# First weights in two halves on SyncE's queue, x tiles 3-4 behind them, and ScalarE's load of tiles 5-6 behind its dummy activation

## The chip, the cores and the metric

The kernel runs on one core of one Trainium2 chip. The metric is the device time of one execution in microseconds. Before the change it is 232.5 us, the median of three runs (232.27, 232.5 and 233.13).

## What is computed

```python
wg = w.reshape(G, M, D)                    # M = 4 weights of a group, along the rows of w
mag = jnp.abs(wg)
order = jnp.argsort(mag, 1)
thr = jnp.take_along_axis(mag, order[:, M - N:M - N + 1, :], 1)   # N = 2: the second largest
mask = (mag >= thr).astype(w.dtype)
wp = (wg * mask).reshape(D, D)
return jnp.einsum("bsd,df->bsf", x, wp) + b
```

x is 16 x 512 x 1024, w is 1024 x 1024, b has 1024 elements, all bf16. In each group of four weights the two of largest magnitude are kept, and x is multiplied by the weights that are left.

## The kernel before, in words

The 8192 rows of x are 64 tiles of 128 rows; w is two row groups g of 512 rows, each laid out as 128 partitions x 4 weights of a group x 1024 columns. Once the weights are pruned and spread into `wp_nat`, the rest of the kernel is plain: x arrives transposed by DMA (`load_nat`, L408), eight matmuls of 128x512 make half a tile of output, VectorE adds the bias and ScalarE's queue stores it.

The start is what the change touches. While the weights are still coming in, tiles 0 to 6 are worked on with the half of x that meets row group 0 (`load_x`, L103): their rows are loaded as they lie, TensorE transposes them four blocks to a tile (`transpose`, L188; the 28 matmuls of L193), ScalarE copies the result to SBUF (`copy_xt`, L196, line L198), and TensorE multiplies by the pruned pieces as they become ready (`mm_piece`, L213, line L229). VectorE prunes a piece in steps (`Piece.do`, L164, lines L169 and L159): the magnitudes (abs), the larger and smaller of each pair (hi, lo), two combinations (t1, t2), the threshold (thr), the mask, and the product (mult). For the first piece, 256 columns of row group 0, some steps stand in parts: abs0a and abs0b are its first and its last two weights of a group, hi0a and hi0b the same, p and q its column halves, y the last two weights, u and v the first and second.

The order on each engine is written out by hand: the lists `order` (L266) hold each engine's steps as tokens, `run` (L391) emits them, and `seq` (L67) chains each engine's instructions in program order. The TensorE list begins T3a T4a T5a T6a T2a, so the transposes of tiles 3, 4, 5, 6 and 2, eight of them for tiles 3-4, eight for 5-6 and four for 2; then come products of tiles 3 and 4 with the first piece, and tiles 0 and 1 are transposed later.

Ahead of the lists stand the loads (L118 to L129). A load is issued from SyncE ("SPq" in the profile, queue q1) or from ScalarE ("ACTq", queue q10). SyncE issues the first two weights of each group of the first piece, then x tiles 3-4, tile 2, the second piece, tiles 0-1 and further weights, and then a transposing DMA (`xlead`). ScalarE issues the last two weights of the first piece and x tiles 5-6. Behind these ScalarE runs a dummy activation into `spark` (L121), in front of which the compiler puts the load of the activation table. Every x or w load above has a semaphore; TensorE's first weight load of tiles 3-4 waits for that of tiles 3-4, and VectorE's two abs steps wait for one half of the first piece each.

TensorE runs fillers before T3a: `filler(6, 4)` makes six matmuls of 512 columns on constants, `filler(14)` fourteen of 128 columns (L404, L405; line L138 in the profile). Their result is not used.

Of the kernel before, what the change touches and what calls it, by code (L numbers as in the profile page):

```python
# [11 lines left out]
def kernel(  # L12
# [7 lines left out]
    nc = tc.nc  # L20
    P = 128
    bf16 = mybir.dt.bfloat16
# [3 lines left out]
    Act = mybir.ActivationFunctionType  # L26
# [28 lines left out]
    const = ctx.enter_context(tc.tile_pool(name="const", bufs=1))  # L55
# [11 lines left out]
    def seq(eng, inst):  # L67
        if eng in tails:
            tc.add_manual_dep(inst.ins, tails[eng].ins.name, NOSYNC, reason="program order")
        tails[eng] = inst  # L70
        return inst

    def pe(i):
        return seq("pe", i)
# [4 lines left out]
    def act(i):  # L79
        return seq("act", i)  # L80
# [4 lines left out]
    def pool(i):  # L85
        return seq("pool", i)

    spark = const.tile([P, 1], bf16)

    w_sb = const.tile([P, G, 4, Dout], bf16)  # L90
    wv = w.rearrange("(g q m) f -> q g m f", g=G, m=4)
    x_sb = {}
# [3 lines left out]
    def issue(eng, out_, in_):  # L96
        q = nc.sync if eng == "sp" else nc.scalar
        return seq(eng, q.dma_start(out_, in_))

    def load_w(g, c0, c1, ma=0, mb=4, eng="sp"):  # L100
        issue(eng, w_sb[:, g, ma:mb, c0:c1], wv[:, g, ma:mb, c0:c1])

    def load_x(ta, tb, eng="sp"):  # L103
        xs = const.tile([P, tb - ta, HK], bf16, name=f"x_{ta}")
        issue(eng, xs[:], xf[ta * P:tb * P, :HK].rearrange("(t p) k -> p t k", p=P))
        for t in range(ta, tb):
            x_sb[t] = xs[:, t - ta, :]
# [8 lines left out]
    xnat, held = {}, {}  # L116

    load_w(0, 0, 256, 0, 2)  # L118
    load_w(0, 0, 256, 2, 4, "act")
    load_x(5, 7, "act")  # L120
    act(nc.scalar.activation(spark[:], nc.const_aps.tensor(1.0, [P, 1], bf16), Act.Abs))  # L121
    load_x(3, 5)
    load_x(2, 3)
    load_w(0, 256, 512)
    load_x(0, 2)
# [10 lines left out]
    def filler(n, rep=1):  # L136
        for _ in range(n):
            pe(nc.tensor.matmul(warm_ps[:, :rep * P], lhsT=nc.const_aps.tensor(1.0, [P, P], bf16),  # L138
                                rhs=nc.const_aps.tensor(1.0, [P, rep * P], bf16), start=True, stop=True))
# [119 lines left out]
    def stage(key):  # L259
        solo = key[1] == "h"  # L260
        q, h, at = (pair_of[key[0]], key[2], int(key[0] != SOLO)) if solo else (key[0], key[1] // 2, key[1] % 2)
        if (q, h) not in staged:
# [12 lines left out]
        ),  # L275
        "dve": (
# [4 lines left out]
        ),  # L281
        "act": (
            "C3a C4a C5a C6a C2a S0b0 C0a C1a abs2 S3b0 S2b0 abs3 S0b1 U6h0 S3b1 S2b1 S0b2 S3b2 S2b2 S0b3 U6h1 S3b3 "
# [107 lines left out]
    def run(queues):  # L391
        while any(queues.values()):
            moved = False
            for eng, toks in queues.items():
                while toks and all(n in written for n in needs(eng, toks[0])):
                    emit(eng, toks[0])
                    tok = toks.pop(0)
                    written.add(tok)
                    if tok[0] == "M" or tok[0].islower():
                        written.update(atoms(tok))  # L400
                    moved = True
            assert moved, queues

    filler(6, 4)  # L404
    filler(14)  # L405
    run({eng: order[eng].split() for eng in order})

    def load_nat(ta, tb):  # L408
# [117 lines left out]
```

## Time and profile before

| | before |
|---|---|
| runs | 232.27, 232.5, 233.13 us |
| profiled execution | 232.89 us |
| its span, first to last instruction | 231.1 us |
| granted TensorE clock, mean | 1.000 |
| TensorE matmuls busy | 226.6 us |
| VectorE busy | 107.9 us |
| ScalarE busy | 14.0 us |
| DMA, mean | 165 GB/s |

All durations in what follows are of the profiled execution, and times are counted from its first instruction. A row of the timeline or of the chain gives start, length, engine, line, operation, output and input, and the number of merged instructions; a trailing bracket gives the idle time before and what ended it. A row of the DMA issues gives the count, the size, and the time from issue to landing. A row of a DMA queue gives packets, MB and the share of 16 engines' time. A row of the stretches gives the stretch, its length, then busy time and number of instructions of TensorE's matmuls, its weight loads, VectorE, ScalarE and GpSimd, then the granted clock, the share of the DMA engines and GB/s. Matmuls are pipelined: each shown length holds the pipeline's depth, so the pace is read from start to start.

### The profile page before, as it was taken

The numbers are of one execution on the slowest core, as the hardware profiler recorded it, in microseconds if no ns is written. First come the engines' busy times: TensorE is split into PE (matmuls) and PEld (weight loads), VectorE is DVE, ScalarE is ACT, GpSimd is POOL, SyncE is SP. The second block draws the span as 40 slices with busy tenths as digits, with TensorE's granted clock in tenths as the row PEclk, the third lists the DMA queues.
The fourth block names the chain that finished last, engine by engine and source line by source line (L and its number), as shares of the span: only waits on it lengthen the run. The fifth ranks groups of instructions, "written<-read, shape, count | busy, mean of one in ns | idle before, by whom it ended". The sixth has DMA issues, their size and how long they took to land.

```text
span 231.1 us, 2851 instructions
## 1 busy us (share of the span) xinstructions
PE 226.6 (98%) x1142; PEld 110.9 (48%) x1162; DVE 107.9 (47%) x200; ACT 14.0 (6%) x27; POOL 17.6 (8%) x15
## 2 busy tenths in 40 slices
PE   8999999999999999999999999999999999999995
PEld 5986444444444444444444444444444444444443
DVE  3999877844424424424424424423423423433434
ACT  2874100000000000000000000000000000000000
POOL 1000199700000000000000000000000000000000
PEclk9999999999999999999999999999999999999999
DMA  6999999997399422991259821693128932122122
GB/s 203 276 197 280 164 217 223 297 320 252 124 206 232 155 91 72 237 281 64 75 116 252 222 94 71 162 298 134 65 91 198 273 122 83 54 91 91 53 86 91
DMA packets 79308, 38.19 MB, mean 165 GB/s; under 512 B 64192, under 2 KB 71744, under 8 KB 79296
## 3 DMA queue, kind: packets, MB, share of 16 engines
q1 hardware_dynamic: 68384, 20.75, 43.6%
q10 hardware_dynamic: 10912, 17.27, 20.9%
q8 instruction: 9, 0.15, 0.3%
q14 instruction: 3, 0.02, 0.0%
HBM read 3.28 MB, written 16.78 MB: 87 GB/s over the span
## 4 chain that ended last, share of the span: by engine, by line
PE 98%; issue 0%; DVE 0%
PE ps L242 88%; PE ps L229 5%; PE tp L242 2%; PE ps L138 2%; PE tp L193 1%; PE ps L193 0%; DVE o L437 0%
## 5 line engine op out<-in xcount | busy, mean ns | idle before, releaser
L242 PE MATMUL ps<-wp_nat,xb 128*128 128x512 bf16 (+1 forms) x831 | 178.9, 375 | 0.9
L242 PEld LDWEIGHTS <-xb 128*128 128x128 bf16 x848 | 82.2, 98 | 97.7
L437 DVE TENSOR_TENSOR o<-ps,bias_sb 128x512 bf16<-128x512 f32 (+1 forms) x112 | 71.6, 677 | 113.7 <-PE ps L242 111.4
L433 POOL TENSOR_TENSOR st<-st,bias_sb 128x1024 f32<-128x1024 f32 x8 | 16.7, 2142 | 0.0
L242 PE MATMUL ps<-wp_nat,xlead 128*128 128x512 bf16 x63 | 14.7, 379 | 0.1
L242 PEld LDWEIGHTS <-xlead 128*128 128x128 bf16 x88 | 8.6, 98 | 10.2
L229 PE MATMUL ps<-wp,xt 128*128 128x256 bf16 (+1 forms) x130 | 12.8, 258 | 0.0
L439 DVE TENSOR_TENSOR o<-ps,st 128x512 bf16<-128x512 f32 x16 | 11.1, 691 | 2.8 <-PE ps L242 2.2
L229 PEld LDWEIGHTS <-xt 128*128 128x128 bf16 x130 | 10.9, 98 | 1.1
L242 PE MATMUL ps<-wp_nat,xlow 128*128 128x512 bf16 x47 | 10.6, 379 | 0.1
L264 ACT COPY st<-ps 128x512 f32<-128x512 f32 x14 | 7.4, 600 | 3.2 <-PE ps L229 3.1
L242 PEld LDWEIGHTS <-xlow 128*128 128x128 bf16 x48 | 4.7, 98 | 5.7
L159 DVE TENSOR_TENSOR mag<-mag,hi 128x256 bf16<-128x256 bf16 (+2 forms) x15 | 6.1, 435 | 0.1
L159 DVE TENSOR_TENSOR wp<-w_sb,mag 128x256 bf16<-128x256 bf16 (+2 forms) x15 | 6.1, 435 | 0.1
L242 PE MATMUL tp<-wp_nat,xlead 128*128 128x512 bf16 x23 | 5.8, 380 | 0.0
L138 PE MATMUL ps<-const-bfloat16-1.0 128*128 128x128 bf16 (+1 forms) x20 | 4.2, 408 | 0.8 <-PEq L510 0.8
L169 DVE TENSOR_SCALAR mag<-w_sb 128x512 uint16<-128x512 uint16 (+2 forms) x5 | 2.3, 473 | 3.5 <-DMA w_sb<-in_w_dram 3.5
L138 PEld LDWEIGHTS <-const-bfloat16-1.0 128*128 128x128 bf16 x20 | 2.3, 146 | 2.4 <-issue 2.4
L159 DVE TENSOR_TENSOR hi<-mag 128x512 bf16<-128x512 bf16 (+2 forms) x7 | 3.2, 458 | 0.1
L159 DVE TENSOR_TENSOR lo<-mag 128x512 bf16<-128x512 bf16 (+1 forms) x6 | 3.1, 509 | 0.0
L193 PEld LDWEIGHTS <-x 128*128 128x128 bf16 x28 | 2.3, 124 | 0.3 <-DMA x<-in_x_dram 0.2
L422 POOL COPY pruned<-wp 128x1 bf16<-128x1 bf16 x1 | 0.2, 187 | 26.7 <-DVE wp L159 26.7
(18 smaller groups left out, 18.8 us busy)
## 6 DMA issues: line engine op xcount, KB each, us to landing
out_dram<-o ACTq DMA_DIRECT2D x58, 256.0 KB, 2.4
wp_nat<-wp SPq DMA_DIRECT2D x14, 128.0 KB, 3.2
out_dram<-o ACTq DMA_DIRECT2D x10, 128.0 KB, 1.7
w_sb<-in_w_dram SPq DMA_DIRECT2D x2, 512.0 KB, 5.5
w_sb<-in_w_dram SPq DMA_DIRECT2D x3, 256.0 KB, 5.1
x<-in_x_dram SPq DMA_DIRECT2D x2, 256.0 KB, 4.3
x<-in_x_dram ACTq DMA_DIRECT2D x1, 256.0 KB, 4.0
bias_sb<-in_b_dram SPq DMA_DIRECT2D x1, 256.0 KB, 4.7
```

Of the source, the lines that this page charges most:

```text
L138: pe(nc.tensor.matmul(warm_ps[:, :rep * P], lhsT=nc.const_aps.tensor(1.0, [P, P], bf16), rhs=nc.const_aps.tensor(1.0, [P, rep * P], bf16), ...
L159: dve(nc.vector.tensor_tensor(out, a, b_, op=op))
L169: dve(nc.vector.tensor_single_scalar(mag.bitcast(u16), w_.bitcast(u16), 0x7FFF, op=Alu.bitwise_and))
L193: pe(nc.tensor.transpose(tp[:, m, :], xg[:, m, :], ident[:]))
L229: pe(nc.tensor.matmul(ps[:, c0 + d:c1 + d], lhsT=xpk[t][:, m, :], rhs=wp[:, g, m, c0:c1], start=(new and m == ms.start), stop=(left[key] = ...
L242: pe(nc.tensor.matmul(ps, lhsT=xt[:, kt - koff, :], rhs=wp_nat[:, kt, c0:c1], start=(kt == first), stop=(kt == last)))
L264: act(nc.scalar.copy(staged[(q, h)][:, at, :, :].rearrange("p t c -> p (t c)"), ps_open.pop(key)[:]))
L422: pool(nc.gpsimd.tensor_copy(out=pruned[:], in_=wp[:, 1, 3, Dout - 1:]))
L433: pool(nc.gpsimd.tensor_tensor(st[:], st[:], bias.to_broadcast([P, 2, 2, CW]), op=Alu.add))
L437: dve(nc.vector.tensor_tensor(o[:, c0:c1], ps, bias_sb[:, c0:c1], op=Alu.add))
L439: dve(nc.vector.tensor_tensor(o[:, c0:c1].rearrange("p (n c) -> p n c", n=2), ps.rearrange("p (n c) -> p n c", n=2), add, op=Alu.add))
```

## The change

The second half of the first piece's weights moves from ScalarE's queue to SyncE's, right behind the first half. Tiles 3-4 follow it on SyncE. ScalarE's first instruction becomes the dummy activation, which now writes one column of the tile that the load of tiles 5-6 fills; so that load waits for it. Three of the 14 short fillers go. VectorE works through abs, hi and lo of the first half before it waits for the second half, and its one lo step of 512 columns becomes two of 256.

```diff
-    spark = const.tile([P, 1], bf16)
...
     def load_x(ta, tb, eng="sp"):
         xs = const.tile([P, tb - ta, HK], bf16, name=f"x_{ta}")
+        if eng == "act":
+            act(nc.scalar.activation(xs[:, 0, :1], nc.const_aps.tensor(1.0, [P, 1], bf16), Act.Abs))
         issue(eng, xs[:], xf[ta * P:tb * P, :HK].rearrange("(t p) k -> p t k", p=P))
...
     load_w(0, 0, 256, 0, 2)
-    load_w(0, 0, 256, 2, 4, "act")
+    load_w(0, 0, 256, 2, 4)
+    load_x(3, 5)
     load_x(5, 7, "act")
-    act(nc.scalar.activation(spark[:], nc.const_aps.tensor(1.0, [P, 1], bf16), Act.Abs))
-    load_x(3, 5)
     load_x(2, 3)
...
         "dve": (
-            "abs0a abs0b hi0a lo0 hi0b t20 t10p t10q thr0p thr0q mask0yp ...
+            "abs0a hi0a lo0a abs0b hi0b lo0b t20 t10p t10q thr0p thr0q mask0yp ...
...
     filler(6, 4)
-    filler(14)
+    filler(11)
```

The rest of VectorE's list, and the lists of the other engines, stay as they are. The load of tiles 5-6 is the only one from ScalarE that `load_x` makes.

8 rows, old and new, of the table order are left out of this document.

## The prediction

> **What bounds the kernel now.** I read the page first, its busy line and its chain of work, and then the chain in order of time and the list of waits for the first 20 us.
>
> ```profile
> PE 226.6 (98%) x1142; PEld 110.9 (48%) x1162; DVE 107.9 (47%) x200; ACT 14.0 (6%) x27; POOL 17.6 (8%) x15
> PE 98%; issue 0%; DVE 0%
> ```
>
> TensorE is busy for 98% of the span, and the chain that ended last runs through it alone.
>
> ```profile
> 0.77 4.21 PE ps L138 x20
> 4.99 1.02 PE tp L193 x8
> ...
> 228.46 0.29 DVE o L437
> ```
>
> These are pieces of that chain (start, length, what). From the first transposes at 4.99 to the last adder at 228.46 the pieces lie end to end. So two things can move the end: the moment at which real work starts on TensorE after the 20 fillers, and a new hole behind it. The list of waits names the one data wait that TensorE has:
>
> ```profile
> PEld L193 <- DMA x<-in_x_dram: 0.2, 1, 0.2
> ```
>
> TensorE's first weight load of x tiles 3-4 waits 0.2 us for their DMA. Now TensorE and VectorE around that start, from the timeline, and the fillers of 128 columns from the groups by form:
>
> ```profile
> L138 PE MATMUL ps<-const-bfloat16-1.0 128*128 128x128 bf16 x14 | 1.7, 314 | 0.0
> 4.96 1.04 PE L193 MATMUL tp<-ident,x 128*128 128x128 bf16 x8
> 5.80 0.72 PE L193 MATMUL ps<-ident,x 128*128 128x128 bf16 x8
> 6.35 0.39 PE L193 MATMUL tp<-ident,x 128*128 128x128 bf16 x4
> 6.58 1.92 PE L229 MATMUL ps<-wp,xt 128*128 128x128 bf16 x20
> 8.33 0.39 PE L193 MATMUL tp<-ident,x 128*128 128x128 bf16 x4
> 3.50 0.49 DVE L169 TENSOR_SCALAR mag<-w_sb 128x512 uint16<-128x512 uint16 x2 [3.50 <-DMA w_sb<-in_w_dram]
> 4.11 0.42 DVE L159 TENSOR_TENSOR lo<-mag 128x512 bf16<-128x512 bf16 x1
> 4.45 0.28 DVE L159 TENSOR_TENSOR hi<-mag 128x256 bf16<-128x256 bf16 x1
> 4.65 0.28 DVE L159 TENSOR_TENSOR lo<-lo 128x256 bf16<-128x256 bf16 x1
> 5.80 0.48 DVE L159 TENSOR_TENSOR wp<-w_sb,mag 128x256 bf16<-128x256 bf16 x2
> ```
>
> A step here is the distance from start to start. A filler steps every (1.7 - 0.314) / 13 = 0.107 us. The first eight transposes step every (5.80 - 4.96) / 8 = 0.105, the next eight every (6.35 - 5.80) / 8 = 0.069, the last four every (6.58 - 6.35) / 4 = 0.057. TensorE thus doubles its pace among transposes 9 to 16: two more steps of 0.107 and six of 0.057 make the 0.55 us, so the change of pace is at about 5.80 + 2 x 0.107 = 6.01. (The granted clock stands at 1.00 in every stretch, one row of them below; only the steps show it.) This decides what an earlier start is worth: a transpose moved ahead of 6.01 still costs 0.107, but takes away only 0.057 behind it.
>
> **The change, part by part.**
>
> *Three fillers fewer.* 3 x 0.107 = 0.32 us. The last of 14 frees TensorE about 0.18 before 4.96, at 4.78; the last of 11 at 4.46. That gains nothing unless x tiles 3-4 land earlier than now.
>
> *The issues.* The two hardware queues now:
>
> ```profile
> 0.73 0.45 SPq L98 DMA_DIRECT2D w_sb<-in_w_dram  x1
> 1.24 0.96 SPq L98 DMA_DIRECT2D x<-in_x_dram  x2
> 0.74 0.50 ACTq L98 DMA_DIRECT2D w_sb<-in_w_dram  x1
> 1.26 0.49 ACTq L98 DMA_DIRECT2D x<-in_x_dram  x1
> 1.79 1.28 ACT L121 ACT_TABLE_LOAD   x1 [1.79 <-issue]
> 3.08 0.20 ACT L121 ACTIVATE spark<-const-bfloat16-1.0 128x1 bf16<-128x1 bf16 x1
> x<-in_x_dram SPq DMA_DIRECT2D x1, 256.0 KB, 3.7
> x<-in_x_dram ACTq DMA_DIRECT2D x1, 256.0 KB, 4.0
> w_sb<-in_w_dram SPq DMA_DIRECT2D x1, 128.0 KB, 2.7
> ```
>
> SyncE takes 0.5 us for each issue (0.73, 1.24, and two more by 1.24 + 0.96 = 2.20). Behind the added half, tiles 3-4 go out at 1.75 in place of 1.24, and every later issue one slot later. ScalarE starts with the table load at about 0.74 instead of 1.79: 0.74 + 1.28 + 0.20 = 2.22, and with the wait on its own activation tiles 5-6 go out at about 2.28 in place of 1.26. Behind that issue ScalarE has only the copies of the transposes, which start at 5.62 now.
>
> *When tiles 3-4 land.* At the latest 1.75 + 3.7 = 5.45 (their own time now, unchanged); at the earliest 1.75 + 2.7 = 4.45 (the time of the first half of the weights, on free DMA engines, with half the bytes). To choose, I look at which queue moved bytes (q1 is SyncE's, q10 ScalarE's) in 2.4-3.0, 3.0-4.0 and 4.0-4.5 us:
>
> ```profile
> q10 hardware_dynamic: 199, 0.10, 54.6%
> q1 hardware_dynamic: 155, 0.08, 45.3%
> ...
> q1 hardware_dynamic: 227, 0.23, 64.3%
> q10 hardware_dynamic: 139, 0.10, 31.4%
> ...
> q10 hardware_dynamic: 156, 0.15, 87.4%
> q1 hardware_dynamic: 50, 0.04, 22.3%
> ```
>
> The queues take turns: q10's half of the weights goes ahead of tiles 3-4, then 0.23 of the 0.26 MB of tiles 3-4 by 4.0, with 0.10 MB of q10 (the end of its weights, and tiles 5-6) among them. The last bytes of tiles 3-4 go near 4.15, and 4.15 + 0.8 is their landing, 1.24 + 3.7 = 4.94. After the change the same 0.26 MB of weights lies ahead of them, but on one queue with the second half sent 0.5 us later; it was through by about 3.1 and I estimate 3.2. Tiles 5-6 cannot be among them before 2.28 + 1.1 = 3.4 (0.73 to the first bytes after 1.8 is 1.1). The 0.26 MB then take 0.26 / 0.36 = 0.7 us at the rate of 3.0-4.5 (0.33 MB in one microsecond, then 0.19 in half of one), to 3.9, and land at about 3.9 + 0.8 = 4.7. I take 4.7, and TensorE starts at 4.75 in place of 4.96.
>
> The Trainium skill, "DMA: Bandwidth & Descriptors", section "Issuing engines are not separate DMA queues", says that transfers issued from SyncE and ScalarE run on the same 16 DMA engines and interleave, and that issuing from several engines saves issue time alone. By that rule the change gives away one issue slot of 0.5 us and its gain from the order of the bytes is small; the rows above, with the two queues taking turns, agree with the sharing.
>
> *When tiles 5-6 land.* At the latest 2.28 + 4.0 = 6.3, at the earliest 2.28 + 2.7 = 5.0. Their bytes now start near 3.5, behind q10's own half of the weights, and end near 4.55 (the 0.15 MB of 4.0-4.5 and little after). Later they are ready at 3.4 and follow tiles 3-4 as now: I take 5.45, 0.2 later than now (1.26 + 4.0 = 5.26). TensorE wants them at 4.75 + 8 x 0.107 = 5.6, so they hold nothing up, by 0.15.
>
> *VectorE.* The second abs waits for the second half of the weights: now it follows the first about 0.2 after 3.50, at 3.7; later its data land at about 1.24 + 2.7 = 3.9. Behind it the chain loses one hi (0.2) and half of a lo (0.33 to 0.2), 0.34 together, so the first products start at 5.80 + 0.2 - 0.34 = 5.66 and end 0.28 later, at 5.9, well ahead of TensorE at 6.5. No cost.
>
> *Everything else on SyncE's queue slides 0.5 us.* Tile 2, the second weights and tiles 0-1 are the first to be missed. These rows say when tiles 0-1 are issued and how long they take, how full the DMA engines are (the last three columns are the granted clock, their share and GB/s), and where SyncE stands later:
>
> ```profile
> 2.96 0.61 SPq L98 DMA_DIRECT2D x<-in_x_dram  x1
> x<-in_x_dram SPq DMA_DIRECT2D x1, 256.0 KB, 5.0
> 5.50:6.00 0.50, 0.50 (x7) 0.50 (x6) 0.50 (x3) 0.38 (x1) 0.00 (x0) 1.00 1.09 330
> 19.37 2.33 SPq L112 DMA_TRANSPOSE xlead<-in_x_dram  x1
> 22.38 1.20 SPq L98 DMA_DIRECT2D wp_nat<-wp  x2
> ```
>
> Tiles 0-1 are issued at 2.96 and land at 7.96; TensorE turns to them at 8.33. The engines are full (1.09), so these bytes queue, and the same bytes lie ahead of them: I take 8.0, and give 7.96 to 8.46 as bounds. TensorE would want them at 8.2. Further on SyncE itself stands idle for VectorE's products, 22.38 - (19.37 + 2.33) = 0.68 us, which swallows a slide of 0.5; up to there the first spread of products is the nearest:
>
> ```profile
> 11.53 3.50 SPq L98 DMA_DIRECT2D wp_nat<-wp  x4
> wp_nat<-wp SPq DMA_DIRECT2D x3, 128.0 KB, 3.6
> 19.46 0.86 PE tp L242 x4
> ```
>
> Its last issue ends by 15.03, and even with 3.6 us from there it lands at 18.6; TensorE wants it at 19.46. A slide of 0.5 leaves 0.3.
>
> *Sum.* From 4.75 to 6.01 go 11.8 slow steps, from 4.96 9.8. Two transposes more are done before the change of pace and take away 2 x 0.057 = 0.11 us behind it. The profiled execution took 232.89 us (span 231.1); it becomes 232.8. It lies 0.4 above the median 232.5, so against the median I say **232.4**.
>
> **The rivals.**
>
> *Tiles 5-6 take over the wait.* At the late bound, 6.3, their first transpose starts at 6.33 in place of 5.80, already at full pace: 12 x 0.057 = 0.68, and the products start at 7.01 in place of 6.58, 0.43 us later: 232.9. For it speaks that their issue waits for 1.5 us of ScalarE's work and that my slack is 0.15; against it that their bytes now wait for other bytes anyway. It decides when they land after 5.6.
>
> *The row on one queue brings nothing.* Tiles 3-4 land at 5.45, TensorE starts at 5.5; 4.8 slow steps, then 15.2 x 0.057 = 0.87, and the products start at 6.88, 0.3 late: 232.8. Tiles 0-1 at 8.46 would cost about the same, 0.2 to 0.3. For it: an issue 0.5 us later; against it: bytes that no longer share.
>
> *Slower: the pace is not raised at 6.01.* The pace rose 6.01 - 0.77 = 5.24 us after the first filler, with one idle stretch of 0.18 us in between. With 11 fillers that stretch is 4.75 - 4.46 = 0.29, or 1.0 if tiles 3-4 land at 5.45. If the hole, or transposes in place of fillers, start the count anew, the pace rises at 4.75 + 5.24 = 9.99; 3.98 us at half pace lose 1.99 us: 234.5. It decides at a hole that is longer than the one of 0.18 that the rows show to be harmless. Nothing here shows how long that is.
>
> The Trainium skill, "TensorE: Matmul & The Clock Gate", section "What's actually happening", has the rise follow a busy window of about 3.4 us that runs freely, so that a spoilt window would cost half of another, an estimate of 1.7 us or 234.2; its section on PE-mode transpose says that transposes do not count as busy in the same way, which speaks against this change. The rows agree with a doubled pace; that it rose amid transposes decides neither.
>
> *Faster by more than that.* The most that the start can give is 4.96 - 4.46 = 0.50 us, were it all at full pace. Only a rise of pace some 2.5 us earlier would give 1.2. The times before already scatter from 232.27 to 233.13.
>
> **How the numbers follow.** 0.5%, or 1.16 us, is about what a measurement of this kernel can tell from no change. Forecast 0.53 (own range 231.9 to 232.8, by the scatter before and tiles 3-4 between 4.45 and 5.1); tiles 5-6 late 0.16; nothing from the row, or tiles 0-1 late, 0.11; pace raised late 0.15; much faster 0.05. Faster 0.05; same 0.53 + 0.16 + 0.11 = 0.80; slower 0.15. The range 231.8 to 233.2 takes in the first three cases with their scatter and leaves out the last two.
>
> **What would show it.** In the timeline after: tiles 3-4 issued at 1.75 and their first transpose near 4.75, still in TensorE's slow steps; ScalarE's issue near 2.28; no wait of TensorE at its second group of transposes (about 5.6); products from about 6.47. A wait for x at the ninth transpose, a first transpose after 5.0, or steps of 0.107 beyond 6.5 would each prove a step wrong.

## The result, and the profile after

The changed kernel takes 233.37 us, the median of 16 runs (232.88 to 234.99); the kernel before takes 232.39 in 16 runs (232.25 to 233.13). The ratio is 1.0041, 95% interval 1.0030 to 1.0052: slower by 0.98 us, within 0.5%, and 0.17 us above the range that I gave. The profiled execution took 233.85 us, its span is 232.1.

The busy line and the chain by engine, from the page of the kernel after:

```profile
PE 228.0 (98%) x1159; PEld 110.6 (48%) x1159; DVE 108.2 (47%) x201; ACT 14.2 (6%) x27; POOL 17.6 (8%) x15
PE 95%; DMA 2%; SPq 1%; issue 0%; DVE 0%
```

TensorE still bounds the kernel, but the chain that ended last no longer begins with fillers: it begins on SyncE's queue and goes through a load of x. In order of time (start, length, what):

```profile
2.76 0.68 SPq L96
3.43 0.04 issue
3.48 5.64 DMA x<-in_x_dram
9.11 0.05 issue
9.16 0.41 PE tp L192 x4
```

The load issued at 3.48 is that of tiles 0-1. It lands at 9.11, and the first transposes of tile 0 start at 9.16; they started at 8.33 before. The timeline of TensorE shows two holes ahead of that:

```profile
4.73 1.04 PE L192 MATMUL tp<-ident,x 128*128 128x128 bf16 x8
5.93 0.86 PE L192 MATMUL ps<-ident,x 128*128 128x128 bf16 x8 [0.16 <-DMA x<-in_x_dram]
6.63 0.39 PE L192 MATMUL tp<-ident,x 128*128 128x128 bf16 x4
6.86 1.92 PE L228 MATMUL ps<-wp,xt 128*128 128x128 bf16 x20
9.16 0.41 PE L192 MATMUL tp<-ident,x 128*128 128x128 bf16 x4 [0.38 <-DMA x<-in_x_dram]
```

Tiles 3-4 came 0.23 us sooner, 4.73 for 4.96. Their eight transposes step every 0.105 and would end at 4.73 + 8 x 0.105 = 5.57, but tiles 5-6 start at 5.93: 0.36 us lost. (The brackets count idle time only after the last matmul has drained, so they show less.) Their own eight transposes then take 6.63 - 5.93 = 0.70 us, 0.25 more than eight of the fast steps of 0.056, since the pace doubles only at 6.5 here. The products start at 6.86 in place of 6.58, and 20 products later TensorE waits again, for tiles 0-1: 6.86 + (8.33 - 6.58) = 8.61 would have been their time, and they came at 9.16.

The issues and landings behind this, from the timeline of SyncE and ScalarE and the DMA issues (us from issue to landing):

```profile
1.74 0.97 SPq L96 DMA_DIRECT2D x<-in_x_dram  x2
2.27 0.45 ACTq L96 DMA_DIRECT2D x<-in_x_dram  x1
x<-in_x_dram SPq DMA_DIRECT2D x1, 256.0 KB, 2.9
x<-in_x_dram SPq DMA_DIRECT2D x1, 128.0 KB, 3.0
x<-in_x_dram ACTq DMA_DIRECT2D x1, 256.0 KB, 3.5
x<-in_x_dram SPq DMA_DIRECT2D x1, 256.0 KB, 5.6
```

Tiles 3-4: 1.74 + 2.9 = 4.7. Tile 2: 2.25 + 3.0 = 5.3, now ahead of tiles 5-6, 2.27 + 3.5 = 5.8; before, tiles 5-6 came first (5.3 against 5.7). Tiles 0-1: 3.48 + 5.6 = 9.1.

**What the end hangs on.** The table puts together the traced execution of every kernel of this study. "Tile 0" is the start of its first transpose, and the last column is the traced time minus it.

| kernel | tiles 3-4 land | tiles 5-6 land | first product | tiles 0-1 land | tile 0 | time | time - tile 0 |
|---|---|---|---|---|---|---|---|
| before | 4.9 | 5.3 | 6.58 | 8.0 | 8.33 | 232.89 | 224.56 |
| before_again | 4.8 | 5.1 | 6.12 | 7.2 | 7.88 | 232.41 | 224.53 |
| after | 4.7 | 5.8 | 6.86 | 9.1 | 9.16 | 233.85 | 224.69 |
| again | 4.8 | 6.0 | 6.98 | 7.8 | 8.73 | 233.27 | 224.54 |
| q_nowait | 5.5 | 4.4 | 7.17 | 7.7 | 8.92 | 233.48 | 224.56 |
| split_wait | 4.4 | 8.0 | 9.36 | 9.3 | 12.77 | 237.54 | 224.77 |
| split_nowait | 4.7 | 5.1 | 6.45 | 7.3 | 8.20 | 232.76 | 224.56 |
| t2_first | 4.7 | 5.8 | 6.48 | 8.4 | 8.43 | 232.99 | 224.56 |
| x56_on_sync | 4.7 | 5.6 | 6.38 | 7.8 | 8.14 | 232.68 | 224.54 |
| x2_on_scalar | 4.7 | 5.5 | 7.26 | 8.0 | 9.01 | 233.55 | 224.54 |
| loads_alone | 4.9 | 6.1 | 6.87 | 8.0 | 8.62 | 233.19 | 224.57 |
| dve_alone | 4.8 | 5.2 | 6.60 | 7.3 | 8.36 | 232.96 | 224.60 |
| hide_56 | 4.8 | 5.9 | 5.97 | 9.5 | 9.57 | 234.14 | 224.57 |
| old_dve | 4.7 | 6.2 | 6.96 | 8.7 | 8.72 | 233.29 | 224.57 |
| slot_alone | 4.6 | 5.0 | 5.91 | 8.3 | 8.35 | 233.06 | 224.71 |
| whole_wait | 4.6 | 6.1 | 6.91 | 8.0 | 8.66 | 233.25 | 224.59 |
| whole_56sync | 4.5 | 6.4 | 7.15 | 8.1 | 8.91 | 233.50 | 224.59 |

In all 17 traces the time is that of tile 0 plus 224.53 to 224.77 us. Whatever the change does to the loads and queues behind it costs at most 0.2 us; what counts is when TensorE turns to tile 0. That is 20 products after the first product, which wait for the transposes of tiles 3 to 6 and 2 and for VectorE, or the landing of tiles 0-1, whichever is later (in hide_56 eight transposes stand among the products). Less 224.6, the medians of 232.39 and 233.37 put tile 0 at about 7.8 before and 8.8 after, an estimate: the median run of the changed kernel is like the trace of "again", not like the first.

### The profile page after: what moved, and what is told of

It is laid out like the page before. It is cut to its first block, busy times and chain, and to the rows that moved or that the text cites. A ratio compares the mean times of both kernels' runs of the same rounds, so it can differ in the third digit from the quotient of the medians.

```text
span 232.1 us, 2867 instructions
## 1 busy us (share of the span) xinstructions
PE 228.0 (98%) x1159; PEld 110.6 (48%) x1159; DVE 108.2 (47%) x201; ACT 14.2 (6%) x27; POOL 17.6 (8%) x15
## 4 chain that ended last, share of the span: by engine, by line
PE 95%; DMA 2%; SPq 1%; issue 0%; DVE 0%
PE ps L241 88%; PE ps L228 5%; DMA x<-in_x_dram 2%; PE tp L241 2%; SPq L96 1%; PE tp L192 0%; DVE o L436 0%; PE ps L192 0%
## 5 line engine op out<-in xcount | busy, mean ns | idle before, releaser
L241 PE MATMUL ps<-wp_nat,xb 128*128 128x512 bf16 (+2 forms) x848 | 179.8, 375 | 0.0
L158 DVE TENSOR_TENSOR lo<-mag 128x512 bf16<-128x512 bf16 (+2 forms) x7 | 3.2, 456 | 0.0
```

The costliest lines, as they stand in the source:

```text
L158: dve(nc.vector.tensor_tensor(out, a, b_, op=op))
L241: pe(nc.tensor.matmul(ps, lhsT=xt[:, kt - koff, :], rhs=wp_nat[:, kt, c0:c1], start=(kt == first), stop=(kt == last)))
```

## The experiments

Three theories from the start: **A**, the slide (the added issue pushes tiles 0-1 back by a slot and the full DMA engines never make it up); **B**, the wait on ScalarE pushes tiles 5-6 among later loads; **C**, the pace (fewer fillers and a hole let TensorE double its pace later). From the first four runs came **D**: tiles 5-6 land last, and TensorE waits for them. Each ratio below is against runs of the kernel before that were taken with it (medians 232.49 to 232.69 us).

### The changed kernel and its two moves of loads, apart

**again**: the changed kernel, no edit.

> The changed kernel once more, for a second trace of it and a time beside the parts. Theory A (slide): the half that was added to SyncE's queue pushes every later load one slot of 0.5 us back, the DMA engines are full from then on, and tiles 0-1 land after TensorE wants them; expects 233.2 to 233.5, tiles 0-1 landing past 8.8 and a wait of TensorE of 0.4 us or more at their first transpose. Theory B (wait on ScalarE): tiles 5-6 go out 1 us later, their bytes fall among those of the second piece and of tiles 0-1; the same here. Theory C (pace): three fillers fewer and the hole behind them let the doubled pace of TensorE come later; expects slow steps of 0.107 up to 6.5 or beyond, and no wait at tiles 0-1 in most runs. A second trace also says whether single DMA packets of 0.5 to 1.9 us, which the first one has, come again.

Measured: 233.44 us, ratio 1.0037 (1.0023 to 1.0050). TensorE's timeline:

```profile
4.85 1.04 PE L192 MATMUL tp<-ident,x 128*128 128x128 bf16 x8 [0.18 <-DMA x<-in_x_dram]
6.13 0.79 PE L192 MATMUL ps<-ident,x 128*128 128x128 bf16 x8 [0.24 <-DMA x<-in_x_dram]
6.75 0.39 PE L192 MATMUL tp<-ident,x 128*128 128x128 bf16 x4
6.98 1.92 PE L228 MATMUL ps<-wp,xt 128*128 128x128 bf16 x20
8.73 0.39 PE L192 MATMUL tp<-ident,x 128*128 128x128 bf16 x4
```

No wait at tiles 0-1 (they land at 7.8), and still as slow as the median: 20 products after 6.98 tile 0 comes at 8.73 without a hole. Here the loss is ahead of the products, at tiles 5-6: 6.13 in place of 4.85 + 8 x 0.107 = 5.71. A alone falls; D comes from this trace. Both signs of C are there too, slow steps up to 6.5 and no wait at tiles 0-1: tiles 5-6 take 6.75 - 6.13 = 0.62 us where eight fast steps take 0.45. So this run loses 0.42 us by waiting and 0.17 by slow steps. No DMA packet of the first 9.5 us took longer than 0.3 us here, against 1.9 in the first trace of the changed kernel.

**q_nowait**: the wait taken out.

```diff
-        if eng == "act":
-            act(nc.scalar.activation(xs[:, 0, :1], ...))
...
     load_x(5, 7, "act")
+    act(nc.scalar.activation(spark[:], ...))
```

> The changed kernel without the wait: tiles 5-6 are issued from ScalarE at 0.74, the dummy activation stands behind the load and writes a tile of its own again; both halves on SyncE, 11 fillers and VectorE's new order stay. A: tiles 0-1 still land past 8.6, 232.9 to 233.4. B: tiles 0-1 at about 8.0 as before the change, 232.2 to 232.5. C: as the changed kernel, 233.2 to 233.5.

Measured: 234.09 us, ratio 1.0069 (1.0045 to 1.0092), above all three ranges. Without the wait tiles 5-6 are first on the engines and land at 4.4, but the two halves of the weights land at 4.0 and 4.8 and tiles 3-4 at 5.5. The first product waits for VectorE until 7.17. So the wait does what it is for, once both halves are on one queue. B's forecast, the time of the kernel before, falls; its mechanism, tiles 5-6 among later loads, lives on in D.

**split_wait**: the wait without the move of the second half.

```diff
-    load_w(0, 0, 256, 2, 4)
+    load_w(0, 0, 256, 2, 4, "act")
```

> The changed kernel with the second half of the weights back on ScalarE, ahead of the dummy activation, so tiles 5-6 go out at about 2.76; SyncE's later loads are one slot earlier again; 11 fillers and VectorE's new order stay. A: tiles 0-1 land at about 8.0; tiles 5-6 land at about 6.3 and hold TensorE up by some 0.5 us instead; 232.7 to 233.0. B: tiles 0-1 late as in the changed kernel or later, 233.2 to 233.8. C: as the changed kernel, 233.2 to 233.5.

Measured: 236.9 us, ratio 1.0167 (1.0133 to 1.0200). All three theories missed it. Tiles 5-6 go out 0.52 later than in the changed kernel, at 2.79, behind the second half of the weights on their own queue, and land 2.2 later, at 8.0: tile 2 (5.3) and the second piece (256 KB, 7.8) land ahead of them. TensorE's timeline:

```profile
4.46 1.06 PE L192 MATMUL tp<-ident,x 128*128 128x128 bf16 x8
8.12 1.02 PE L192 MATMUL ps<-ident,x 128*128 128x128 bf16 x8 [2.60 <-DMA x<-in_x_dram]
9.36 3.62 PE L228 MATMUL ps<-wp,xt 128*128 128x128 bf16 x20
13.20 0.41 PE L228 MATMUL ps<-wp,xt 128*128 128x256 bf16 x2
13.67 2.54 PE L228 MATMUL ps<-wp,xt 128*128 128x256 bf16 x33
```

After a hole of 2.6 us the 20 products, 1.92 to 2.00 us long in the other traces that run them in a row, take 3.62: slow steps to about 13.3. So the mechanism of my slower rival exists, at a hole of 2.6 us ahead of which the pace had not yet risen.

**split_nowait**: the kernel before with `filler(11)` and VectorE's new order; no load moved.

> The kernel before with 11 fillers in place of 14 and VectorE's new order alone; all loads as before the change. A and B: 232.3 to 232.5, nothing lost, since TensorE waits for tiles 3-4 at 4.96 either way. C: 232.9 to 233.4, the slow steps lasting to 6.5 or beyond.

Measured: 232.85 us, ratio 1.0012 (1.0004 to 1.0021): 0.3 us are lost, more than A and B have and just less than C. But the pace doubles at 5.6 in this trace, not at 6.5 or later, so C's reason does not show; dve_alone, below, says where the loss is likely to lie.

### Tiles 5-6: their place in the row, and work in the hole

**t2_first**: tile 2 transposed ahead of tiles 5-6.

```diff
-            "T3a T4a T5a T6a T2a M3.0yp ...
+            "T3a T4a T2a T5a T6a M3.0yp ...
...
-            "C3a C4a C5a C6a C2a ...
+            "C3a C4a C2a C5a C6a ...
```

> The changed kernel with tile 2 transposed and copied ahead of tiles 5-6 on TensorE and ScalarE; all loads as in the changed kernel. Theory D (tiles 5-6 last): the loss is TensorE's wait of 0.4 us for tiles 5-6, which land at 5.8 to 6.0 behind tile 2 at 5.2 to 5.3; the four transposes of tile 2 now fill the hole, 4 x 0.057 to 4 x 0.107: products 0.25 us earlier, 233.1 to 233.25. Theory A (slide): nothing changes at tiles 0-1, 233.4 to 233.5.

Measured: 233.14 us, ratio 1.0027 (1.0018 to 1.0036). As D expects, though the interval still overlaps that of the changed kernel. In its trace the products start at 6.48, but tile 0 only at 8.43, tiles 0-1 having landed at 8.4: the second wait stands right behind the first.

**x56_on_sync**: tiles 5-6 on SyncE, ahead of tile 2.

```diff
-    load_x(5, 7, "act")
+    load_x(5, 7)
+    act(nc.scalar.activation(spark[:], ...))
     load_x(2, 3)
```

> The changed kernel with the load of tiles 5-6 on SyncE, behind tiles 3-4 and ahead of tile 2; ScalarE keeps only the dummy activation, into a tile of its own. D: tiles 5-6 are issued at 2.25 as now, but ahead of tile 2 and the second piece; they land at 5.2 to 5.4, no hole at the ninth transpose, products at 6.3 to 6.6: 232.6 to 232.9. A: every load behind slides another slot of 0.5 us, tiles 0-1 hold TensorE up more often: 233.5 to 234.

Measured: 233.03 us, ratio 1.0024 (1.0006 to 1.0041), one run of 12 at 235.12.

```profile
5.68 0.64 PE L193 MATMUL ps<-ident,x 128*128 128x128 bf16 x8 [0.33 <-DMA x<-in_x_dram]
6.38 1.92 PE L229 MATMUL ps<-wp,xt 128*128 128x128 bf16 x20
```

Issued at the same time as in the changed kernel, 2.25, but ahead of tile 2, tiles 5-6 land at 5.6 in place of 5.8 to 6.0. The place in the row counts, but it recovers less than half: the pace had doubled before the transposes in this trace, and TensorE still waits for tiles 5-6. The median is 0.13 above what I expected. A is refuted: tiles 0-1, issued at 4.00, two slots late, land at 7.8.

**x2_on_scalar**: tile 2 behind tiles 5-6 on ScalarE, SyncE's later loads back in their old slots.

```diff
-        if eng == "act":
+        if eng == "act" and ta == 5:
...
-    load_x(2, 3)
+    load_x(2, 3, "act")
```

> The changed kernel with the load of tile 2 on ScalarE's queue behind tiles 5-6; SyncE's second piece, tiles 0-1 and the rest are one slot earlier, as before the change. D: tiles 5-6 no longer share with tile 2, but with the second piece that follows on SyncE; landing 5.5 to 5.9, 232.8 to 233.3. A: the slide is undone, tiles 0-1 land in time in every run, 232.4 to 232.7.

Measured: 233.63 us, ratio 1.0045 (1.0032 to 1.0058), above both ranges. Tiles 5-6 land at 5.5, but now the second piece goes ahead of tile 2, which lands at 7.0; TensorE waits for tile 2 and the first product starts at 7.26. A is wrong here: with the slide undone the kernel is not faster. The wait moved to tile 2, now issued last of the three.

**before_again**: the kernel before, for a second trace.

> The kernel before once more, for a second trace. It is to show what differs between its runs of 232.25 and those of 233.1: theory C (pace) says the moment at which the steps halve, so a run near 232.4 has it 0.5 to 1 us ahead of the 6.01 of the first trace, and its products start between 6.0 and 6.3 in place of 6.58.

Measured: 232.41 us. TensorE's timeline:

```profile
4.80 0.82 PE L193 MATMUL tp<-ident,x 128*128 128x128 bf16 x8
5.46 0.61 PE L193 MATMUL ps<-ident,x 128*128 128x128 bf16 x8
5.90 0.39 PE L193 MATMUL tp<-ident,x 128*128 128x128 bf16 x4
6.12 1.92 PE L229 MATMUL ps<-wp,xt 128*128 128x128 bf16 x20
7.88 0.39 PE L193 MATMUL tp<-ident,x 128*128 128x128 bf16 x4
```

Tiles 5-6 already step by (5.90 - 5.46) / 8 = 0.055: the pace doubled before 5.46, not at 6.01, and the products start 0.46 earlier than in the first trace. That is the difference between a run of 232.4 and one of 232.9. The first trace, on which I predicted, was a late one.

### The other parts alone

**loads_alone**: the changed kernel with `filler(14)` and VectorE's old order.

> The changed kernel with 14 fillers and VectorE's old order: the moved loads and the wait are all that is left of the change. D (tiles 5-6 last): TensorE still waits for tiles 5-6 until 5.8 to 6.0 and the products start at 6.8 to 7.0: 233.2 to 233.5, the whole loss. C (pace, fillers): three fillers more close the hole ahead of the first transposes, so part of the loss is gone, 232.6 to 233.0.

Measured: 233.19 us, ratio 1.0026 (1.0016 to 1.0037), first product at 6.87. Most of the loss is in the moved loads and their wait. The remaining 0.1% lies inside the two intervals and stays unassigned.

**dve_alone**: the kernel before with VectorE's new order.

> The kernel before with VectorE's new order alone (abs, hi and lo of the first two weights, then of the last two), 14 fillers, all loads as before. If the 0.3 us that the kernel with 11 fillers and this order lost came from the order, this one is at 232.75 to 232.95 too, with no run under 232.6, since the first products of weights come at 6.1 in place of 5.8; if it came from the fillers, 232.4 to 232.6.

Measured: 232.89 us, ratio 1.0009 (1.0000 to 1.0018), lowest run 232.68. TensorE and, behind it, VectorE:

```profile
5.80 0.39 PE L193 MATMUL tp<-ident,x 128*128 128x128 bf16 x4
6.60 0.61 PE L229 MATMUL ps<-wp,xt 128*128 128x128 bf16 x8 [0.41 <-DVE wp L159]
6.26 0.48 DVE L159 TENSOR_TENSOR wp<-w_sb,mag 128x256 bf16<-128x256 bf16 x2
```

With both halves landing together, the new order brings the first product of weights at 6.26 in place of 5.80, and TensorE waits for it. So the order costs when nothing is gained at the first half; it is the likely source of split_nowait's 0.3 us, though this interval reaches down to 1.0000.

**hide_56**: the changed loads, VectorE's old order, and tiles 5-6 transposed only after the first eight products.

```diff
-            "T3a T4a T5a T6a T2a M3.0yp M4.0yp M3.0yq M4.0yq M5.0y M6.0y M3.0u M4.0u M3.0v M4.0v M6.0u ...
+            "T3a T4a T2a M3.0yp M4.0yp M3.0yq M4.0yq T5a T6a M3.0u M4.0u M3.0v M4.0v M5.0y M6.0y M6.0u ...
...
-            "C3a C4a C5a C6a C2a ...
+            "C3a C4a C2a C5a C6a ...
```

> The changed kernel with VectorE's old order and with tiles 5-6 out of the way: TensorE transposes tiles 3, 4 and 2, multiplies tiles 3 and 4 by the last two weights, and only then transposes tiles 5-6; the loads and 11 fillers stay. D (tiles 5-6 last): no wait for tiles 5-6 is left, TensorE is bound by the first products of weights at 5.9 to 6.0; the work ahead of tile 0 ends 0.3 to 0.5 us earlier than in the changed kernel: 232.5 to 232.8. A (slide): 233.4 as the changed kernel, with a wait at tiles 0-1.

Measured: 233.12 us, ratio 1.0028 (1.0014 to 1.0042). The traced run is the slowest of its 12, 234.14:

```profile
5.97 0.61 PE L228 MATMUL ps<-wp,xt 128*128 128x128 bf16 x8
6.41 0.61 PE L192 MATMUL ps<-ident,x 128*128 128x128 bf16 x8
6.86 1.51 PE L228 MATMUL ps<-wp,xt 128*128 128x256 bf16 x12
9.57 0.41 PE L192 MATMUL tp<-ident,x 128*128 128x128 bf16 x4 [1.21 <-DMA x<-in_x_dram]
```

The wait for tiles 5-6 is gone, and TensorE stands ready for tile 0 at 8.2; tiles 0-1 land at 9.5. D was right about the first wait and blind to the second: no more than 0.3 us comes back. At the median of 233.12 tile 0 would start at about 8.5 (less 224.6, an estimate), so a wait of some 0.3 us at tiles 0-1 is likely in the typical run too.

**old_dve**: the changed kernel with VectorE's old order alone.

> The changed kernel with VectorE's old order alone, 11 fillers and the new loads. If tiles 5-6 hold TensorE up, the products of weights are early enough in both orders and nothing changes: 233.2 to 233.5. If VectorE's new order is part of the loss, as in the kernel before with this order alone, 232.9 to 233.1.

Measured: 234.12 us, ratio 1.0080 (1.0056 to 1.0103), six runs from 233.29 to 235.22; the traced one, 233.29, waits 0.9 us at tiles 5-6. Neither expectation holds: the median is 0.9 above that of loads_alone, which has three fillers more, and the trace, of the fastest run, does not say why. Two more kernels with a long wait in their traces, q_nowait (1.2 us) and whole_wait (0.8), have runs at 235 to 236. The wait alone does not make such runs: whole_56sync waits 1.25 us for tiles 5-6, and its six runs end at 234.09. The granted clock on record is lower in some of them: 0.993 in the run of 235.22 here and 0.991 to 0.993 in the three of whole_wait at 236.0 to 236.2, where 0.7% of 235 us is 1.6 us. It is 1.00 in the run of 235.01 and in those of q_nowait; a late first doubling would not show in it, for split_wait's traced run of 237.54 has 0.999. So the lower pace is shown for some of these runs and open for the rest.

### What delays tiles 0-1

**slot_alone**: the kernel before with one nearly empty issue on SyncE.

```diff
     load_x(2, 3)
+    slot = const.tile([P, 16], bf16)
+    issue("sp", slot[:], w[0:P, 0:16])
     load_w(0, 256, 512)
```

> The kernel before with one more issue on SyncE, a load of 16 columns of w (4 KB) into a tile that nothing reads, between tile 2 and the second piece; all later loads of SyncE go out 0.5 us later, as in the changed kernel. Slot theory: tiles 0-1 land at 8.0 to 8.8 and TensorE waits for them in part of the runs, 232.7 to 233.1. Row theory: the engines are full anyway, tiles 0-1 land at 7.3 to 8.0 as before, 232.4 to 232.6.

Measured: 233.17 us, ratio 1.0025 (1.0015 to 1.0034). TensorE, the load of tiles 0-1, issued at 3.44, and two stretches (the last three columns are the granted clock, the DMA engines' share and GB/s):

```profile
5.91 1.92 PE L231 MATMUL ps<-wp,xt 128*128 128x128 bf16 x20
8.35 0.41 PE L195 MATMUL tp<-ident,x 128*128 128x128 bf16 x4 [0.53 <-DMA x<-in_x_dram]
x<-in_x_dram SPq DMA_DIRECT2D x1, 256.0 KB, 4.9
5.50:6.00 0.50, 0.50 (x11) 0.42 (x9) 0.50 (x4) 0.50 (x3) 0.00 (x0) 1.00 0.74 185
6.50:7.00 0.50, 0.50 (x7) 0.45 (x5) 0.50 (x3) 0.07 (x1) 0.00 (x0) 1.00 0.64 170
```

The earliest products of all traces, 5.91, and then a hole: 20 products would end at 5.91 + 1.75 = 7.66, and tiles 0-1 land at 8.3. One issue slot of 0.5 us, with 4 KB behind it, costs 0.6 us at the median. The 4 KB themselves are small: their 128 packets took 1.2 us together, spread over 16 engines. So the row theory falls, and the added issue is enough for a loss. How it delays tiles 0-1 is open. The DMA engines were not full: their share is 0.74 and 0.64 in the two stretches, and 1.09 and 1.02 in the kernel before. And the slot alone does not set the landing: issued at 3.44 to 3.48, tiles 0-1 landed anywhere from 7.7 to 9.5 in eight traces.

**whole_wait**: both halves in one load on SyncE.

```diff
-    load_w(0, 0, 256, 0, 2)
-    load_w(0, 0, 256, 2, 4)
+    load_w(0, 0, 256)
```

> The changed kernel with both halves of the first weights in one load on SyncE (256 KB), so that tiles 3-4 and all later loads go out 0.5 us earlier, in the old slots; tiles 5-6 still wait for the dummy activation; VectorE in its old order, 11 fillers. Slot theory: tiles 0-1 land at 7.3 to 8.0; what is left is the wait for tiles 5-6, which now fall behind the second piece as well, landing past 6: 233.0 to 233.6. Row theory: tiles 0-1 past 8.3 in spite of the earlier issue, 233.4 or more.

Measured: 233.81 us, ratio 1.0066 (1.0035 to 1.0097). The load of 256 KB takes 0.75 us to issue, so half of the slot is lost again; tiles 0-1 land at 8.0 and hold nothing up in this trace. Tiles 5-6 land at 6.1, as the slot theory has it, and the first product starts at 6.91. The landings are those of the slot theory; the median is 0.2 above its range.

**whole_56sync**: the same, tiles 5-6 on SyncE and tile 2 on ScalarE behind the dummy activation.

> The same with tiles 5-6 on SyncE behind tiles 3-4, and tile 2 on ScalarE behind the dummy activation: weights at 0.73, tiles 3-4 at 1.3, tiles 5-6 at 1.8, the second piece at 2.3. If the two waits are the whole loss, tiles 3-4 land at 4.6 and tiles 5-6 at 5.2 and the products are bound by VectorE at 6.0 to 6.2: 232.3 to 232.6, as before the change or a little faster. If tile 2, issued at 2.27, falls behind the second piece as it did when it followed tiles 5-6 on ScalarE, it lands at 6 to 7 and holds TensorE up: 232.8 to 233.6.

Measured: 233.76 us, ratio 1.0051 (1.0038 to 1.0065). This is above both ranges. Tiles 5-6, issued at 2.12 right behind tiles 3-4, land at 6.4 where I had 5.2, and tile 2 at 6.6; the first product starts at 7.15. The place in the row does not explain that landing; the DMA engines moved 160 GB/s between 4.0 and 4.5 here, and 363 in the half microsecond before. No version with the weights on one queue came out ahead of the kernel before. So no run removes both waits, and that the two are the whole loss is not shown.

## Why the prediction was wrong

By its steps:

- **Fillers and tiles 3-4: right.** Landing forecast 4.7, measured 4.69; transposes forecast 4.75, measured 4.73 (4.85 in the second trace). But this gain is small: before_again has its transposes at 4.80 with the old loads.
- **Tiles 5-6: the step that failed.** I took 5.45, "0.2 later than now", and a slack of 0.15. They land at 5.8, 6.0, 6.1 and 6.2 in the traces that have all the moved loads and TensorE's old order, and in the two of the changed kernel TensorE loses 0.36 and 0.42 us to the wait that I put at nothing. I had them follow tiles 3-4 directly; tile 2, on SyncE's queue, goes ahead of them, and x56_on_sync shows 5.6 where it does not. That is still 0.2 after my 5.45. A second term that my sum lacks is the slow stretch of the DMA engines between 3.0 and 3.5 us (last section); what each of the two is worth was not separated. My first rival had the right wait and point of decision (5.6), and I gave it 0.16. Its price of 0.43, against 6.98 - 6.58 = 0.40 in "again", is close by luck: it has a landing at 6.3 and the pace already doubled.
- **Tiles 0-1: failed as well, in part of the runs.** I took 8.0, with 8.46 as the upper bound. They landed at 8.7, 9.1 and 9.5 in three of the traces with a later slot, and at 8.3 in slot_alone, where a slot of 4 KB makes TensorE lose 0.7 us; "again" has 7.8 and no wait. My reason, that the engines are full and the bytes queue, held in the trace that I read and not in slot_alone. I treated the two late loads as alternatives of 0.2 to 0.4 us. They stand one behind the other: whoever removes the first (t2_first, hide_56) meets the second, and gets back 0.3 us at most.
- **The pace: the sum was built on one run.** The doubling at 6.01 belongs to that execution: it is before 5.46 in before_again and at 6.5 in the first two traces of the changed kernel. (The views show a granted clock of 1.00 all along; the clock record packed in these four traces begins only at the doubling, at 6.02 and 5.25 before and at 6.49 and 6.54 after.) The kernel before has its products at 6.1 in a run of 232.4, and against that run the changed kernel loses much more than against the late one that I worked from: 6.98 - 6.12 = 0.86 us, 0.17 of it slow steps, against 6.98 - 6.58 = 0.40. So a difference that is read from a late run cannot be taken off the median, as my last line did. Even the lowest runs differ by 232.88 - 232.25 = 0.63.
- **The slower rival**, a late doubling, was not the main cause. In the two traces of the changed kernel the pace doubles 0.4 to 0.6 us after the hole at tiles 5-6, so that hole does not start the count anew, and the slow steps behind it cost 0.17 and 0.25 us, not 1.99. Nor do 11 fillers make it late: in the eight other traces that have them and both halves of the weights on SyncE it comes between 3.6 and 5.8. split_wait shows the effect at 2.6 us. The Trainium skill, "TensorE: Matmul & The Clock Gate", section "What's actually happening", gives a freely running window of about 3.4 us. The traces agree with that: but for split_wait the doublings, from 3.6 to 6.5 us, spread over less than one such window, and the stretches of full clock on record are 221.87, 225.28 or 228.69 us long, which differ by 3.41. The slow pace behind split_wait's long hole agrees with it too. The earliest doubling, at 3.6, comes 2.8 us after the first filler, less than one window.
- **VectorE: half right, and close by luck.** I had the first products of weights at 5.66; they came at 5.77. The second half landed at 3.46 where I had 3.9, and the steps from the second abs (3.77) to the products took 2.00 us where I had 1.76. Three rows show why the steps took longer:

```profile
3.03 0.29 DVE L168 TENSOR_SCALAR mag<-w_sb 128x512 uint16<-128x512 uint16 x1 [3.03 <-DMA w_sb<-in_w_dram]
3.36 0.29 DVE L158 TENSOR_TENSOR hi<-mag 128x256 bf16<-128x256 bf16 x1
3.57 0.28 DVE L158 TENSOR_TENSOR lo<-mag 128x256 bf16<-128x256 bf16 x1
```

  A step that reads what the step right before it wrote follows after 0.33 us, one that does not after 0.21, and the new order has more of the first kind. It cost nothing in the changed kernel, since tiles 5-6 were later; dve_alone shows its price.
- **The queues behind: right.** Time minus tile 0 is 224.5 to 224.6 before and 224.5 to 224.7 after.

## What to carry to other kernels

When a start-up is bound by several loads in a row, write down for each load what is issued ahead of it on every queue and when its consumer turns to it; here, where one load was helped (t2_first, hide_56, x2_on_scalar), the wait went to another. An issue slot of half a microsecond ahead of a load can cost as much even when it carries 4 KB, and DMA engines that look full in one trace need not be full in the next. And a start that depends on TensorE's pace needs more than one trace: here the same kernel starts its products 0.46 us apart from run to run.

## What the runs showed of the hardware

Between 3.0 and 3.5 us, about where the loads on one queue pass from the weights to tiles 3-4, the DMA engines of the changed kernel moved little; first the kernel before, then the one after:

```profile
DMA packets 174, 0.14 MB, mean 275 GB/s; under 512 B 12, under 2 KB 174, under 8 KB 174
```

```profile
DMA packets 57, 0.05 MB, mean 90 GB/s; under 512 B 6, under 2 KB 57, under 8 KB 57
```

This was not expected and its cause is open, but it belongs to the moved loads. In the eight traces where the two halves and tiles 3-4 are three loads in a row on SyncE and ScalarE's first load, if there is one, goes out at 2.26 or later (after, again, t2_first, x56_on_sync, x2_on_scalar, loads_alone, hide_56, old_dve), the engines moved 65 to 120 GB/s between 3.0 and 3.5. In the nine others they moved 275 to 369. At 300 GB/s or more that is some 0.1 MB, or 0.3 us, lost ahead of everything behind it, an estimate. And a load that was issued 0.52 us later landed 2.2 us later (2.27 to 5.8 in the changed kernel, 2.79 to 8.0 in split_wait, one trace each); two loads of another queue landed ahead of it there, one in the changed kernel.
